# A two-layer transformer kernel whose first attention unit is worked in two parts of keys, with other constants in its ordering program

## The chip, the cores and the metric

The kernel runs on one core of a Trainium2 chip. A core has a matrix engine (TensorE, PE in the profile), a vector engine (VectorE, DVE), a scalar engine for activation functions (ScalarE, ACT), a general engine (GpSimd, POOL), and a queue that here issues all DMA transfers (SyncE, SP). Each engine works through its own instructions in order and waits on semaphores for the others. The metric is the time of one execution in microseconds on the device. Lower is better.

## The reference

Two layers of attention and gated feed-forward with the same weights, over 2048 tokens of width 512, with 32 heads of 16 channels:

```python
def _A_ref(x, wqkv, wo):
    qkv = (x @ wqkv).reshape(B, S, 3, H, Dh).transpose(2, 0, 3, 1, 4)
    q, k, v = qkv[0], qkv[1], qkv[2]
    scores = jnp.einsum("bhqd,bhkd->bhqk", q, k) * (Dh ** -0.5)
    p = _softmax(scores, axis=-1)
    o = jnp.einsum("bhqk,bhkd->bhqd", p, v)
    return o.transpose(0, 2, 1, 3).reshape(B, S, D) @ wo

def _B_ref(x, w_gate, w_up, w_down):
    return (_gelu(x @ w_gate) * (x @ w_up)) @ w_down

x = x + _A_ref(_layernorm(x), A_wqkv, A_wo)
x = x + _B_ref(_layernorm(x), B_w_gate, B_w_up, B_w_down)
x = x + _A_ref(_layernorm(x), A_wqkv, A_wo)
x = x + _B_ref(_layernorm(x), B_w_gate, B_w_up, B_w_down)
```

B is 1, S 2048, D 512, H 32, Dh 16, and the feed-forward is 1792 wide. All inputs and the output are bf16.

## The kernel before, in words

Everything stays on the chip between the first load and the last store. The attention is cut into units: four heads (a group, g from 0 to 7) and a block of 512 tokens as queries (256 in the last two blocks of the second layer). Unit 0 is the first group of the first block. Each unit is worked in two passes over all keys.

Pass 1 finds the row maxima that the softmax needs. TensorE multiplies 128 queries by 512 keys of one head (line 1648), using 32 rows of its array, so that heads lie in row groups of their own. VectorE reduces one or two such PSUM banks to a maximum for each query (line 1663) and writes it into `PM`. A unit of 512 queries has 64 such pieces: 4 tiles of queries, 4 blocks of keys and 4 heads. When all are there, `fin` or `fin_pool` (line 987) takes the maximum over the blocks into `MSEL`, VectorE transposes it into `MT`, and `negmax` (line 1027) has SP move it with four small DMAs (line 1040) into an extra row of `QT`. The scores of pass 2 thus come with the maximum already subtracted.

Pass 2 multiplies 128 keys by the 512 queries (line 1518), ScalarE takes the exponential of one or two banks (line 1494) into `SCR`, and TensorE multiplies that by the values with a column of ones (line 1542), adding up in PSUM bank 7. `nrm` then copies and divides.

There is a third way for part of pass 1, the fold: GpSimd subtracts one key block from another (`kd`, line 1279), TensorE multiplies by the difference (line 1467), ScalarE applies a relu (line 1474), and VectorE adds that to the other block's scores while taking the maximum, in one custom instruction (line 1658). Two blocks are thus done with one reduction on VectorE and one relu on ScalarE.

Around this lie layer norms, projections for keys, queries and values (line 671), transposes (line 816), evacuations of PSUM (line 686 on VectorE, 688 on ScalarE), the output projection, and the feed-forward.

The order of all instructions is worked out in Python when the kernel is built. The program keeps a clock for each engine and at each step chooses what TensorE issues next: the next piece of pass 1, the next pieces of pass 2, both, a piece of a projection or feed-forward, a PV product, or a filler. A filler (line 1687) multiplies zeros into unused columns of a bank, and is issued when TensorE's load over the last 3.4 us falls below a bound. Another sort, the "silent" fillers, fill the gap up to the next event without being counted on the program's clock; they are issued while that clock is between 12 us and `HF`, and only while TensorE is in full-array mode. They share line 1687's matmul.

The choices are steered by 21 constants, among them how far pass 1 may lead before the evacuations go to VectorE (`LAGT`), how far it may lead before a fold is wanted (`FL`), how many tiles of pass 2 go in one step (`NT`), and how much full-array work is cut into one piece (`PIECE`). `PLAN` has one row of these for each 16 steps of pass 1's position; 129 rows cover the run. Reading a row:

```python
SPC, SPLIT, S1C, S2C, OV, LIM, NT, P2B, LAG, LAGT, FL, GL, FX, AHD, DUE, DUEM, PIECE, GP, NPV, PB, OVF = PLAN[stretch[0]]
```

Some units can be split over the keys. Pass 1 of a split unit gives the maximum over its first `n_part` key blocks early (`fin_part`, VectorE reduction and transpose at lines 938 and 940), so that pass 2 can work through those keys; the sums of that part are kept (`keep_part`, line 1059) and later scaled by the exponential of the difference of the two maxima (`merge`, lines 967 to 975) and added (line 1090). Before, the first three units of layer 2 are split, and by `TSPL` the last unit. `HSPL` would split unit 0:

```python
        if HSPL:
            split[0] = 0
            n_part[0] = HNA
            extra[0] = n_qt - 1
```

`HNA` is 3, so the first part has three of four key blocks. `extra` names a second slot of `QT`, into which GpSimd copies the unit's queries (`q_copy`), so that both parts have their maximum in a slot of their own.

Of the kernel before, what the change touches and what calls it, by code (L numbers as in the profile page):

```python
# [310 lines left out]
def _build(nc, x_in, wqkv, wo, wg, wu, wd, out, layer_blocks=((512, 512, 512, 512), (512, 512, 512, 256, 256)),  # L311
# [16 lines left out]
    with es:  # L328
# [1369 lines left out]
        while True:  # L1698
# [3 lines left out]
            if pos["p1"] >= STRETCH * stretch[0]:  # L1702
                if stretch[0] < len(PLAN):
                    SPC, SPLIT, S1C, S2C, OV, LIM, NT, P2B, LAG, LAGT, FL, GL, FX, AHD, DUE, DUEM, PIECE, GP, NPV, PB, OVF = PLAN[stretch[0]]
# [34 lines left out]
            if SP and seam != was[0]:  # L1739
                keep_piece, PIECE = (PIECE, SP) if seam else (0, keep_piece)  # L1740
# [189 lines left out]
```

## Time and profile before

| | |
|---|---|
| median of three runs | 2525.06 us (2524.16 to 2528.22) |
| the profiled execution | 2523.95 us |
| its span, first to last instruction | 2522.2 us |
| granted clock of TensorE | 1.000 |
| TensorE / VectorE / ScalarE / GpSimd busy | 2409.2 / 2403.7 / 2353.2 / 683.9 us |

The profile records one execution. Busy time is the time in which an engine had an instruction under way. Groups are named by line, engine, operation, output and input; "idle before" is the engine's idle time ahead of the group's instructions, and the arrow names what ended it. Neighbouring instructions overlap a little in the records, so a row's mean is some 0.08 us longer than the distance between two in a chain. A line of the table of stretches gives start and end, length, and then the busy time and number of instructions of TensorE, its weight loads, VectorE, ScalarE and GpSimd, the granted clock, and the DMA share and rate.

### The profile page before, as it was taken

What the parts mean: (1) busy time and instruction counts of PE and PEld (TensorE: products, weight loads), DVE (VectorE), ACT (ScalarE), POOL (GpSimd) and SP (SyncE); (2) the same over time, 40 slices, a digit from 0 to 9 for tenths busy, and PEclk for the clock granted to TensorE, in tenths of its full rate; (3) what the DMA queues carried; (4) which work ended last, traced back from release to release, by engine and by line L of the source; (5) the groups of instructions that cost most, each with busy time, mean ns of one, the idle gap of its engine ahead of it and who ended that gap; (6) DMA issues with size and microseconds to landing.
All of it is one profiled execution on the core that took longest, in us unless ns stands there. A gap on an engine that the chain in (4) does not pass through costs nothing.

```text
span 2522.2 us, 68091 instructions
## 1 busy us (share of the span) xinstructions
PE 2409.2 (96%) x29682; PEld 1161.1 (46%) x29881; DVE 2403.7 (95%) x3131; ACT 2353.2 (93%) x3267; POOL 683.9 (27%) x1119
## 2 busy tenths in 40 slices
PE   8999999999999999999999999999999999999999
PEld 3444443445434444344434455434453445534556
DVE  7999999999999999999998999999999999999973
ACT  7799999999999999999979899999999999989996
POOL 4111223321332213431133311341113311442300
PEclk9999999999999999999999999999999999999999
DMA  3110000000000000000000000000000000000000
GB/s 102 38 56 6 4 9 2 4 2 2 8 1 4 2 4 6 3 3 14 13 3 4 17 2 2 8 4 10 2 4 6 6 6 3 4 3 14 2 7 6
DMA packets 27419, 25.07 MB, mean 10 GB/s; under 512 B 9456, under 2 KB 26096, under 8 KB 27120
## 3 DMA queue, kind: packets, MB, share of 16 engines
q1 hardware_dynamic: 27120, 20.71, 2.9%
q8 instruction: 234, 3.83, 0.7%
q14 instruction: 65, 0.53, 0.1%
HBM read 9.70 MB, written 2.10 MB: 5 GB/s over the span
## 4 chain that ended last, share of the span: by engine, by line
PE 42%; DVE 32%; ACT 24%; issue 1%; POOL 0%; ACTq 0%
DVE PM L1663 30%; ACT SCR L1494 22%; PE PS L1648 14%; PE PS L671 12%; PE PS L1542 9%; PE PS L1687 4%; PE PS L1518 3%; ACT SCR L1474 1%; DVE SCR L1658 1%; PE PS L816 1%; ACT AO L1114 0%; PE PS L1467 0%; ACT XNT L688 0%; ACT ATTT L688 0%; ACT SG L688 0%
## 5 line engine op out<-in xcount | busy, mean ns | idle before, releaser
L1663 DVE TENSOR_REDUCE PM<-PS 128x1 f32<-128x512 f32 (+1 forms) x2513 | 2216.6, 944 | 52.0 <-PE PS L1518 24.1
L1494 ACT ACTIVATE SCR<-PS 128x1024 bf16<-128x1024 f32 (+1 forms) x2533 | 2008.2, 899 | 59.2 <-PE PS L1518 43.4
L1648 PE MATMUL PS<-KT,QT 32*128 32x512 bf16 x3923 | 1013.1, 384 | 49.4 <-DVE PM L1663 31.9
L1518 PE MATMUL PS<-QT,KT 32*128 32x512 bf16 (+1 forms) x4608 | 924.0, 360 | 7.5 <-ACT SCR L1494 6.3
L1542 PE MATMUL PS<-VP,SCR 128*128 128x51 bf16 (+1 forms) x16384 | 800.8, 187 | 12.3 <-ACT SCR L1494 8.0
L1542 PEld LDWEIGHTS PS<-VP,SCR 128*128 128x128 bf16 x16384 | 568.3, 96 | 486.8 <-issue 424.8
L1648 PEld LDWEIGHTS PS<-KT,QT 32*128 32x128 bf16 x3923 | 242.2, 91 | 547.8 <-DVE PM L1663 324.5
L1687 PE MATMUL PS<-WV,ZER 128*128 128x240 bf16 x2425 | 425.2, 266 | 4.7 <-ACT SCR L1494 4.5
L1096 POOL TENSOR_TENSOR RL<-ACCS,CM 128x16 f32<-128x16 f32 (+1 forms) x63 | 174.5, 2769 | 564.5 <-ACT ACCS L1086 564.3
L1518 PEld LDWEIGHTS PS<-QT,KT 32*128 32x128 bf16 x4608 | 230.2, 91 | 69.3 <-ACT SCR L1494 42.5
L1687 PEld LDWEIGHTS PS<-WV,ZER 128*128 128x128 bf16 x2425 | 185.1, 96 | 63.9 <-issue 48.5
L1242 POOL TENSOR_TENSOR HT<-HT,AO 128x512 bf16<-128x512 bf16 (+1 forms) x107 | 119.5, 1119 | 236.9 <-ACT AO L1240 236.9
L996 POOL TENSOR_TENSOR PM<-PM 128x16 f32<-128x16 f32 (+2 forms) x130 | 30.2, 232 | 379.1 <-DVE PM L1663 373.9
L1279 POOL TENSOR_TENSOR KD<-KT 128x512 bf16<-128x512 bf16 x72 | 82.9, 1152 | 173.9 <-PE PS L1467 166.0
L671 PE MATMUL PS<-XNT,WU 128*128 128x512 bf16 (+1 forms) x447 | 116.3, 353 | 7.3 <-issue 6.2
L671 PE MATMUL PS<-WD,HT 128*128 128x512 bf16 x381 | 115.5, 380 | 7.2 <-issue 5.4
L671 PE MATMUL PS<-XNT,WG 128*128 128x512 bf16 (+1 forms) x488 | 116.3, 357 | 3.6 <-ACT HT L1221 2.1
L1116 POOL TENSOR_TENSOR X<-X,AO 128x512 f32<-128x512 f32 x46 | 58.3, 1266 | 218.8 <-ACT AO L1114 218.8
L1658 DVE CUSTOM_DVE_ANT_0 SCR<-PS,SCR 128x512 bf16<-128x512 f32 x173 | 111.7, 685 | 3.1 <-PE PS L1467 0.6
L1474 ACT ACTIVATE SCR<-PS 128x512 bf16<-128x512 f32 (+1 forms) x121 | 97.1, 802 | 18.7 <-PE PS L1467 18.3
L1221 ACT ACTIVATE HT<-PS 128x512 bf16<-128x512 f32 (+1 forms) x126 | 69.3, 550 | 36.2 <-PE PS L671 33.4
L671 PEld LDWEIGHTS PS<-XNT,WG 128*128 128x128 bf16 x504 | 39.2, 97 | 55.0 <-issue 29.6
(111 smaller groups left out, 991.0 us busy)
## 6 DMA issues: line engine op xcount, KB each, us to landing
KT<-SG SPq DMA_DIRECT2D x64, 64.0 KB
QT<-MT SPq DMA_DIRECT2D x236, 1.0 KB
QT<-SG SPq DMA_DIRECT2D x56, 64.0 KB
out_dram<-AO SPq DMA_DIRECT2D x16, 128.0 KB, 1.7
WG<-in_B_w_gate_dram SPq DMA_DIRECT2D x4, 448.0 KB, 4.8
WU<-in_B_w_up_dram SPq DMA_DIRECT2D x4, 448.0 KB, 4.7
WD<-in_B_w_down_dram SPq DMA_DIRECT2D x4, 384.0 KB, 4.7
QT<-MT SPq DMA_DIRECT2D x68, 0.5 KB
```

What stands on the lines that cost most here:

```text
L671: ins = e.matmul(out_ap, lhsT=l, rhs=r_, start=(i == 0), stop=(i == n - 1))
L1096: emit("pool", lambda e: e.tensor_tensor(RL[:, s, 0:4 * nq], lsum, CM1[:, 0:4 * nq], op=ALU.pow), r=[("ACCS", s), ("CM1",)], w=[("RL", s)] ...
L1242: emit("pool", lambda e, ft=ft, o=o: e.tensor_tensor(HT[:, ft, 0:n], HT[:, ft, 0:n], AO[:, o, 0:n], op=ALU.mult), r=[("AO", o), ("HT", ft) ...
L1279: emit("pool", lambda e: e.tensor_tensor(KD[:, s, :], KT[:, g, ka * 512:(ka + 1) * 512], KT[:, g, kb * 512:(kb + 1) * 512], op=ALU.subtrac ...
L1474: emit("act", lambda e: e.activation(PT[:, s0:s0 + cnt, :], PS[:, bk:bk + cnt, :], ACTF.Relu), r=bks, w=[("PT", s0 + d) for d in range(cnt ...
L1494: emit("act", lambda e: e.activation(dst, src, ACTF.Exp, scale=DH ** -0.5), r=[BK[bk + i] for i in range(cnt)], w=[("PT", i) for i in slot ...
L1518: ins = e.matmul(bank(bk)[:, i * n:(i + 1) * n], lhsT=KT[32 * j:32 * j + 32, g, kt * 128:(kt + 1) * 128], rhs=QT[32 * j:32 * j + 32, s, 0: ...
L1542: ins = e.matmul(acc, lhsT=PT[:, slot, i * n + qt * 128:i * n + (qt + 1) * 128], rhs=AP(VP, (kt * H + 4 * g + j) * 17, [[NTT * H * 17, 128 ...
L1648: ins = e.matmul(bank(b), lhsT=QT[32 * j:32 * j + 32, s, qt * 128:(qt + 1) * 128], rhs=KT[32 * j:32 * j + 32, g, kb * 512:(kb + 1) * 512], ...
L1658: emit("dve", lambda e, i=i, b=b, sl=sl: e.tensor_tensor_reduce(PT[:, sl, :], bank(b), PT[:, sl, :], 1.0, -3.0e38, ALU.add, ALU.max, po[:, ...
L1663: emit("dve", lambda e: e.tensor_reduce(po, PS[:, bs[0]:bs[0] + cnt, :], axis=AX.X, op=ALU.max), r=bks, w=[("PM", sm) + h[1:] for h in hs] ...
L1687: return e.matmul(PS[:, b, NACC:512], lhsT=ZER[:, :], rhs=WV[:, 0, 0:512 - NACC], start=(b != 7), stop=(b != 7), skip_group_check=True)
```

## The change

Unit 0 is split: its pass 2 can begin with the first 1536 keys once their maxima are there, and its last 512 keys follow as a second part, with the maximum over all keys. The silent fillers are allowed up to 100 us of the program's clock, 60 before. And 106 of the 129 rows of `PLAN` have other constants, some in one of 21, some in nearly all; 23 rows are unchanged. No other code differs.

```diff
 PLAN = [
-    (0.1, 0.1, 0.45, 0.42, 0.3, -0.05, 1, 1, 62, 84, 8, 60, 0.3, 2.0, 0, 2, 2, 1, 7, 1, 0.0),
-    (0.1, 0.1, 0.45, 0.42, 0.3, -0.05, 2, 1, 62, 84, 8, 60, 0.1, 2.0, 0, 2, 2, 2, 7, 1, -0.1),
-    (0.0, 0.1, 0.45, 0.42, 0.3, -0.05, 2, 1, 62, 84, 8, 60, 0.1, 2.0, 0, 2, 2, 2, 7, 1, -0.1),
-    (0.2, 0.1, 0.55, 0.42, 0.3, -0.05, 1, 0, 22, 84, 8, 20, 0.3, 2.0, 0, 6, 1, 2, 9, 1, 0.0),
...
+    (0.1, 0.1, 0.45, 0.42, 0.3, -0.05, 2, 1, 62, 84, 8, 60, 0.3, 2.0, 0, 2, 2, 1, 7, 1, 0.0),
+    (0.1, 0.1, 0.45, 0.22, 0.3, -0.05, 2, 1, 62, 84, 8, 60, 0.3, 2.0, 0, 2, 2, 1, 7, 1, 0.0),
+    (0.15, 0.15, 0.45, 0.42, 0.3, -0.05, 1, 1, 78, 84, 8, 50, 0.3, 2.0, 0, 2, 2, 2, 7, 1, 0.0),
+    (0.2, 0.1, 0.55, 0.82, 0.3, -0.05, 1, 0, 22, 84, 8, 30, 0.4, 2.0, 0, 6, 1, 2, 9, 1, 0.0),
...
-    (0.1, 0.15, 0.45, 0.42, 0.3, 0.05, 1, 1, 94, 92, 8, 60, 0.3, 2.0, 0, 2, 2, 2, 11, 1, 0.0),
-    (0.15, 0.2, 0.25, 0.32, 0.5, -0.05, 1, 1, 86, 84, -2, 80, -0.1, 2.0, 10, -14, 2, 1, 9, 1, 0.0),
...
+    (0.1, 0.15, 0.45, 0.42, 0.3, 0.0, 3, 1, 78, 84, 8, 60, 0.7, 2.5, 10, 2, 2, 2, 3, 1, 0.1),
+    (0.2, 0.15, 0.45, 0.42, 0.3, 0.0, 3, 1, 78, 84, 8, 60, 0.7, 3.5, 10, 2, 2, 2, 3, 1, 0.1),
...
 def _build(nc, x_in, wqkv, wo, wg, wu, wd, out, layer_blocks=((512, 512, 512, 512), (512, 512, 512, 256, 256)),
-           ... NSPL=3, HSPL=0, TSPL=1, HNA=3, TNA=3, ... HV=16, TW=0.95, HF=60, VS=14, ...):
+           ... NSPL=3, HSPL=1, TSPL=1, HNA=3, TNA=3, ... HV=16, TW=0.95, HF=100, VS=14, ...):
```

Where `HV` is named: with unit 0 split, the value projections of the first 12 tiles of keys are due 16 steps of pass 1 earlier.

More of the change, by code (lines that the diff above doesn't have):

```diff
@@ L311, in _build @@
 def _build(nc, x_in, wqkv, wo, wg, wu, wd, out, layer_blocks=((512, 512, 512, 512), (512, 512, 512, 256, 256)),
-           n_ahead=6, n_pre=6, S1C=0.45, S2C=0.42, OV=0.3, PD=80, FDUE=20, LIM=-0.05, NT=1, AHD=2.0, DUEM=2, FDL2=0, OPD=12, URG=0.3, ft_tok=512, n_pt=8, n_qt=8, SPLIT=0.15, SPC=0.1, PVC=47, WARM=0.55, WARML=0.42, NPV=7, BOOST=0.0, LAG=62, LAGT=84, GP=2, SING=0, DUE=0, END=360, LAGE=10, FD=205, FDL=-10, QD=32, KD_=16, VD=20, FL=8, FMAX=6, NKD=2, FLOOK=2, FX=0.3, GF=1, NSPL=3, HSPL=0, TSPL=1, HNA=3, TNA=3, PB=1, OVF=0.0, LNP=0, FNP=1, NSG=3, LNT=12, HV=16, TW=0.95, HF=60, VS=14, SO=1.0, SF=1, SP=0, FAST=1, TG=0, GS=2, P2B=1, PIECE=2, GL=60, GLE=20, HARD=-1e9):
+           n_ahead=6, n_pre=6, S1C=0.45, S2C=0.42, OV=0.3, PD=80, FDUE=20, LIM=-0.05, NT=1, AHD=2.0, DUEM=2, FDL2=0, OPD=12, URG=0.3, ft_tok=512, n_pt=8, n_qt=8, SPLIT=0.15, SPC=0.1, PVC=47, WARM=0.55, WARML=0.42, NPV=7, BOOST=0.0, LAG=62, LAGT=84, GP=2, SING=0, DUE=0, END=360, LAGE=10, FD=205, FDL=-10, QD=32, KD_=16, VD=20, FL=8, FMAX=6, NKD=2, FLOOK=2, FX=0.3, GF=1, NSPL=3, HSPL=1, TSPL=1, HNA=3, TNA=3, PB=1, OVF=0.0, LNP=0, FNP=1, NSG=3, LNT=12, HV=16, TW=0.95, HF=100, VS=14, SO=1.0, SF=1, SP=0, FAST=1, TG=0, GS=2, P2B=1, PIECE=2, GL=60, GLE=20, HARD=-1e9):
     S = x_in.shape[1]
```

192 rows, old and new, of the table PLAN are left out of this document.

## The prediction

> **What bounds the kernel now.** I read the page's busy shares first, then the busy time in stretches of 100 us, then the head in finer stretches, then ScalarE's and VectorE's rows there.
>
> ```profile
> PE 2409.2 (96%) x29682; PEld 1161.1 (46%) x29881; DVE 2403.7 (95%) x3131; ACT 2353.2 (93%) x3267; POOL 683.9 (27%) x1119
> ...
> L1663 DVE TENSOR_REDUCE PM<-PS 128x1 f32<-128x512 f32 (+1 forms) x2513 | 2216.6, 944 | 52.0 <-PE PS L1518 24.1
> L1494 ACT ACTIVATE SCR<-PS 128x1024 bf16<-128x1024 f32 (+1 forms) x2533 | 2008.2, 899 | 59.2 <-PE PS L1518 43.4
> L1687 PE MATMUL PS<-WV,ZER 128*128 128x240 bf16 x2425 | 425.2, 266 | 4.7 <-ACT SCR L1494 4.5
> ```
>
> Two engines are nearly full side by side: VectorE with the row maxima of pass 1 (L1663), ScalarE with the exponentials of pass 2 (L1494). TensorE's 96% contain 425 us of fillers (L1687), so it has room. Idle is 2522.2 - 2403.7 = 118.5 us on VectorE and 169.0 us on ScalarE. The stretches say where:
>
> ```profile
> 0.00:100.00 100.00, 85.75 (x594) 36.93 (x599) 81.19 (x119) 71.94 (x121) 30.70 (x67) 1.00 0.24 69
> 100.00:200.00 100.00, 95.38 (x1313) 49.84 (x1313) 99.18 (x142) 98.23 (x110) 18.83 (x37) 1.00 0.16 55
> 200.00:300.00 100.00, 96.86 (x1283) 49.26 (x1281) 98.65 (x145) 99.26 (x112) 18.02 (x40) 1.00 0.02 6
> ...
> 2400.00:2522.00 122.00, 115.91 (x1556) 69.70 (x1558) 68.73 (x109) 95.36 (x143) 6.56 (x13) 1.00 0.02 7
> ```
>
> The columns are PE, PEld, DVE, ACT, POOL, the granted clock and DMA. The head leaves VectorE 18.8 and ScalarE 28.1 us idle, the last 122 us 53.3 and 26.6; between them the two run at 96 to 99%. So time is gained only where an idle stretch of one is filled and the gain is shared with the other. ScalarE's timeline has the head's largest hole:
>
> ```profile
> 72.02 0.60 ACT L688 ACTIVATE SG<-PS 128x512 bf16<-128x512 f32 x1 [1.13 <-PE PS L671]
> 74.09 1.02 ACT L1474 ACTIVATE SCR<-PS 128x1024 bf16<-128x1024 f32 x1 [1.48 <-PE PS L1467]
> 76.68 1.02 ACT L1474 ACTIVATE SCR<-PS 128x1024 bf16<-128x1024 f32 x1 [1.56 <-PE PS L1467]
> 83.40 5.71 ACT L1494 ACTIVATE SCR<-PS 128x1024 bf16<-128x1024 f32 x7 [5.69 <-PE PS L1518]
> 89.59 22.37 ACT L1494 ACTIVATE SCR<-PS 128x1024 bf16<-128x1024 f32 x24 [0.48 <-PE PS L1518]
> ```
>
> The first exponential starts at 83.40 and ScalarE is then full. It waits for the maxima of unit 0 over all 2048 keys, taken apart on GpSimd, transposed and moved into QT:
>
> ```profile
> 74.78 0.25 POOL L996 TENSOR_TENSOR PM<-PM 128x32 f32<-128x32 f32 x1 [9.88 <-DVE PM L1663]
> ...
> 78.19 0.20 DVE L1000 STREAM_TRANSPOSE MT<-MSEL 128x32 bf16<-128x32 bf16 x1
> ...
> 78.42 2.43 SPq L1040 DMA_DIRECT2D QT<-MT  x4
> ```
>
> The stretches of the head:
>
> ```profile
> 63.60:69.00 5.40, 5.40 (x25) 1.35 (x24) 4.12 (x6) 3.88 (x6) 1.23 (x3) 1.00 0.10 26
> 69.00:83.40 14.40, 12.68 (x85) 5.51 (x83) 14.25 (x25) 3.42 (x6) 2.65 (x8) 1.00 0.08 20
> 83.40:100.00 16.60, 15.71 (x214) 8.35 (x213) 16.55 (x25) 15.95 (x19) 0.00 (x0) 1.00 0.00 1
> ```
>
> From 69 to 83.4 VectorE is full (14.25 of 14.40) and ScalarE works 3.42.
>
> **The split of unit 0.** Unit 0 takes its key blocks one after the other. VectorE's timeline shows four bursts with gaps before 40.31, 53.11 and 64.61, about 9.8 us of maxima each; the third ends at 63.65, the fourth near 74.7. With the split the maxima of the first 1536 keys suffice. Added at once on VectorE: a reduction and a transpose, which the layer turn's split units show at 0.21 each (L938, L940), so MT is ready at 64.1. From MT to the first score took 78.39 to 82.88, or 4.5 us, through four DMAs of 0.61; the first exponential followed 0.5 us later. The part's first exponential thus falls at 69.1, 14.3 us earlier. Other conditions: the values of key tiles 0 to 11 (12 evacuations VP end by 53.6) and a copy of QT on GpSimd (nearest row: 1.15 us for a 512-wide L1279), hidden since GpSimd works 3.9 of 19.8 us there.
>
> What is queued behind the new steps: on SP the four DMAs (2.43 us) stand in a run of 16 key moves, 50.32 to 73.74; the moves behind them belong to later groups, so I cost them at nothing. If that cover is gone, a key move is 2.4 us late and pass 1 with it. On TensorE scores and PV of the part come among the last four key projections (68.8 to 72.0), 0.6 us each; those slip into 72 to 83.4, where fillers take about 6 us.
>
> ScalarE's gain: idle 14.40 - 3.42 = 11.0 us, and 0.48 before 89.59, makes 11.4; the part's 24 exponentials at 0.93 (22.37/24) are 22.4 us of work, enough to fill it. Added on ScalarE: keeping the part (L1059, 0.39) and one small exponential (L970, 0.21), so 10.8 net. Added on VectorE: 0.42 for the part, 0.21 for the full maximum that GpSimd did before, so 0.63. GpSimd gets 0.22 + 0.66 + 0.76 of merging (L967, L975, L1090) and loses 1.5 of the tree; it is 27% busy, nothing.
>
> What the 10.8 us are worth depends on sharing. A fold costs ScalarE a relu (0.92 in the chain) and spares VectorE two paired maxima at 1.14 for two custom instructions at 0.61: 1.06 saved. With x us of folds, ScalarE ends 10.8 - x earlier and VectorE 1.16x - 0.63; equal at x = 5.3, both 5.5 us earlier (about 6 more relus, 12 more custom rows than the 173). Ends: no sharing, and VectorE alone counts, +0.6; ScalarE alone is the bound, as the chain has it from 92 to 112 us, -10.8. I take **-5.5**, since both are at 98 to 99% from 100 to 300 us.
>
> [...] Rows first: two full-array projections among row-tiled scores take 0.54 us in the chain of waits, while fourteen in a row took 3.13, 0.45 for two; with one score matmul the round is 0.86. [...]
>
> **Fillers to 100 us instead of 60.** They go only into idle gaps of TensorE in full-array mode. From 60 to 100 us TensorE is idle 2.8 us in all, the longest gap 0.71, and the granted clock is 1.00 in every stretch. Nothing to gain; at worst each of some 26 fillers of 0.1 delays real work, +2.8. I take 0, the longest gap holding six of them.
>
> **The constants.** 106 of 129 rows differ, 65 of them in no more than five of 21 constants; their means hardly move (tiles at once 1.85 to 1.88, lag 49.4 to 47.2). No row prices this. Its field is the idle between head and tail, 46 us on VectorE and 114 on ScalarE, and how often VectorE takes one bank instead of two: 1276 single maxima at 0.680 against 1237 double ones at 1.216. The nearest stretch is the layer turn, 1240 to 1420 us, 15.1 and 28.7 us idle, mean 22; rows 65 and 66 (counted from 0) are replaced in 16 of 21 constants. Halving or doubling half of that gives -11 and +11. I take **-2**, a tenth of that mean; it is a choice and little more.
>
> **Sum.** The profiled execution took 2523.95 (span 2522.2 and 1.75 around it); -5.5 + 0 - 2.0 gives 2516.5. The median of the three runs is 1.1 above it, so I forecast 2517.5 against 2525.06. No change is what lies within 0.2% (5 us), about what a measurement of this kernel tells apart: 2520.0 to 2530.1.
>
> **Rivals.**
> - *ScalarE's head start stays with ScalarE.* It reaches the maxima sooner and waits there: the wait of L1494 for scores (43.4 us in all) grows by some 10. VectorE's 0.6 is then the sum: 2525.7. For it: only 121 relus in the whole run. Against it: ScalarE at 99% up to 300 us.
> - *The part does not start early,* because its DMAs or the scores wait behind the key moves and projections before 72 us; half the gain and a little delay of pass 1: 2522 to 2525. TensorE is 100% busy in 63.6:69. [...]
> - *The constants find more:* half the turn's idle goes: 2525.06 - 5.5 - 11 = 2508.5.
> - *Slower.* One mechanism: a step of the order puts pass-2 matmuls ahead of the next pair of maxima, and VectorE waits for them; in the rows, L1663 after L1518 is 24.1 us over 66 waits. Where three tiles go at once instead of one (rows 19 and 20 are changed so), each step holds VectorE longer. VectorE is nearly full, so what it waits more is added: with the -5.5 kept, the change is slower than 2530 once these waits grow by 10.5, and by two thirds of their size, 16 us, it takes 2525.1 - 5.5 + 16 = 2535.6. Against it: the mean of that constant hardly moves.
>
> **Chances.** The forecast's mechanism 0.45 (own range 2511 to 2523, of it 0.05 above 2520); first rival 0.13; second 0.07; third 0.15; slower 0.20. Faster: 0.40 + 0.15 = 0.55. Same: 0.05 + 0.13 + 0.07 = 0.25. Slower 0.20. The range 2505 to 2536 takes most of the third and half of the slower case and leaves some 0.15 out; cases of both signs together hold it.
>
> **What would show it.** A reduction of 128x16 from 128x48 near 63.7 us, four moves QT<-MT near 64.2, the first L1494 near 69 instead of 83.40, ScalarE over 12 of 14.4 us busy from 69 to 83.4, and some 185 custom maxima. If these hold and the custom rows don't grow while the wait of L1494 does, sharing failed. If VectorE's idle after L1518 grows past 34 us, the constants did it. Were the first exponential later than 75 us, the second rival holds; a time over 2530 would make the forecast wrong in sign.

## The result, and the profile after

The changed kernel takes 2529.44 us (median of 20 runs, 2526.34 to 2538.93), the kernel before 2524.75 (20 runs beside them, 2523.78 to 2528.22). The ratio is 1.0019, with a 95% interval of 1.0012 to 1.0025. The change is slower by 4.7 us. That is inside the 5 us which the prediction called no change, but the interval excludes no change, and the forecast was 2517.5. The profiled execution took 2530.99 us, with a span of 2529.3 and a mean granted clock of 0.998.

In some profiled executions the granted clock of TensorE falls to 0.50, as for 3.4 us at 56 us or for 10.2 us at 2488; that other long runs with a lower mean clock have such a fall is inferred from the two numbers. Of the 20 runs five are at 2526.3 to 2527.1, seven at 2528.7 to 2529.5 and eight at 2531.0 or more; the mean clock goes down with them, from 1.000 to 0.995. Of the 20 of the kernel before, 16 are near 2524.6 and four near 2528.2. The profiled execution of the changed kernel has such a fall; that of the kernel before has none.

The busy line of the changed kernel's page, and rows of its groups of instructions (columns as before):

```profile
PE 2412.8 (95%) x29669; PEld 1160.4 (46%) x29871; DVE 2402.3 (95%) x3162; ACT 2360.1 (93%) x3285; POOL 680.8 (27%) x1117
...
L1663 DVE TENSOR_REDUCE PM<-PS 128x1 f32<-128x512 f32 (+1 forms) x2516 | 2207.6, 939 | 49.6 <-PE PS L1518 18.3 <-PE PS L1648 13.4 <-PE PS L1467 2.1
L1494 ACT ACTIVATE SCR<-PS 128x1024 bf16<-128x1024 f32 (+1 forms) x2548 | 2012.2, 896 | 64.5 <-PE PS L1518 47.1 <-PE PS L1467 0.3
...
L1658 DVE CUSTOM_DVE_ANT_0 SCR<-PS,SCR 128x512 bf16<-128x512 f32 x183 | 118.0, 686 | 2.8 <-PE PS L1648 1.1 <-PE PS L1518 0.3
...
L1474 ACT ACTIVATE SCR<-PS 128x512 bf16<-128x512 f32 (+1 forms) x127 | 103.0, 812 | 18.5 <-PE PS L1467 17.7 <-PE PS L1648 0.5
```

The two rows of the fold in the kernel before, which the prediction gave only as counts:

```profile
L1658 DVE CUSTOM_DVE_ANT_0 SCR<-PS,SCR 128x512 bf16<-128x512 f32 x173 | 111.7, 685 | 3.1 <-PE PS L1467 0.6 <-PE PS L1648 0.4 <-PE PS L1518 0.2
...
L1474 ACT ACTIVATE SCR<-PS 128x512 bf16<-128x512 f32 (+1 forms) x121 | 97.1, 802 | 18.7 <-PE PS L1467 18.3
```

There are ten more custom maxima and six more relus (the prediction had 12 and 6). VectorE's maxima and custom maxima together are 2.7 us less (9.0 less and 6.3 more); ScalarE is busy 6.9 us more. VectorE's wait for pass-2 scores went down, from 24.1 to 18.3 us: the mechanism that the prediction named for "slower" did not occur.

**The head start came as forecast.** The timeline of the changed kernel, one line each of VectorE, SP's queue and ScalarE:

```profile
64.07 0.21 DVE L938 TENSOR_REDUCE MSB<-PM 128x16 bf16<-128x48 f32 x1
...
64.55 2.42 SPq L1040 DMA_DIRECT2D QT<-MT  x4
...
69.53 1.02 ACT L1494 ACTIVATE SCR<-PS 128x1024 bf16<-128x1024 f32 x1 [1.49 <-PE PS L1518]
```

The first exponential starts at 69.53 instead of 83.40, and ScalarE fills part of the hole (the fourth busy time):

```profile
69.00:83.40 14.40, 14.15 (x125) 5.72 (x126) 13.74 (x22) 10.67 (x18) 0.00 (x0) 1.00 0.09 22
83.40:100.00 16.60, 16.59 (x187) 8.08 (x186) 16.41 (x31) 14.00 (x18) 1.22 (x3) 1.00 0.01 2
```

It works 10.67 us from 69 to 83.4, where it worked 3.42; the prediction had asked for over 12. And it is no longer full behind that: 14.00 of 16.60, before 15.95.

**The gain stopped at the next unit's maxima.** When unit 0's pass 2 is done, ScalarE needs the maxima of unit 1. GpSimd's first step of taking them apart, before and after:

```profile
106.71 0.25 POOL L996 TENSOR_TENSOR PM<-PM 128x32 f32<-128x32 f32 x1 [28.86 <-DVE PM L1663]
```

```profile
106.70 0.25 POOL L996 TENSOR_TENSOR PM<-PM 128x32 f32<-128x32 f32 x1 [18.48 <-DVE PM L1663]
```

They are ready at the same time to 0.01 us. Unit 1's first exponential follows at 114.93, within 0.1 us of unit 0's last; before, it came at 115.19. The last copy of unit 0's sums (L1086) ends at 117.2, before 116.5. So 13.9 us of head start are gone 47 us later. ScalarE's rows from 69 to 114.5 us, each shape by itself, before:

```profile
L1494 ACT ACTIVATE SCR<-PS 128x1024 bf16<-128x1024 f32 x30 | 28.5, 1065 | 6.3 <-PE PS L1518 6.2
L1474 ACT ACTIVATE SCR<-PS 128x1024 bf16<-128x1024 f32 x3 | 3.1, 1046 | 3.0 <-PE PS L1467 3.0
L1494 ACT ACTIVATE SCR<-PS 128x512 bf16<-128x512 f32 x4 | 2.5, 620 | 0.0
```

and after:

```profile
L1494 ACT ACTIVATE SCR<-PS 128x1024 bf16<-128x1024 f32 x23 | 21.8, 1038 | 2.6 <-PE PS L1518 2.5
L1494 ACT ACTIVATE SCR<-PS 128x512 bf16<-128x512 f32 x18 | 10.5, 595 | 4.3 <-PE PS L1518 4.1
L1474 ACT ACTIVATE SCR<-PS 128x1024 bf16<-128x1024 f32 x6 | 6.1, 1032 | 0.4 <-PE PS L1467 0.3
```

The exponentials are 64 banks in both, but now 18 are taken one at a time: 32.3 us of work instead of 31.0, and 6.9 us of waiting instead of 6.3. Three more relus take 3.0 us. With 0.6 for keeping and scaling the part, ScalarE is busy 5.2 us more in this stretch (39.11 against 33.87 of 45.50); the other 6 of the 11.4 us stay idle, in smaller pieces. It waits for scores there, though TensorE has room: fillers take 9.9 of its 22.8 busy us from 69 to 92. VectorE got four more custom maxima for unit 1 (14 against 10 up to 106.7, some 2.1 us spared at the forecast's price), and lost nearly as much by beginning unit 1 at 76.01 instead of 74.61 and by 0.5 us more of idle time up to 106.7.

**Behind the head the two passes drift apart.** The end of each unit's pass 2 (L1086), after minus before: +0.7 us at 117, between -2.8 and +1.0 up to 1100, -6.0 at 1439, -2.0 at 1828, +1.4 at 1990, +2.7 at 2475. The last transpose of pass 1 ends at 2456.4, where it ended at 2470.7. So pass 1 gains 14 us and pass 2, which ends the kernel, loses 2.7. The stretches near the end, before:

```profile
2456.00:2472.00 16.00, 15.45 (x253) 8.49 (x252) 13.41 (x20) 16.00 (x19) 0.40 (x1) 1.00 0.01 2
2472.00:2490.00 18.00, 17.64 (x259) 10.16 (x258) 0.20 (x1) 17.54 (x31) 0.98 (x3) 1.00 0.01 2
```

and after:

```profile
2456.00:2472.00 16.00, 15.36 (x249) 8.50 (x247) 0.52 (x3) 16.00 (x19) 0.40 (x1) 1.00 0.01 2
2472.00:2490.00 18.00, 17.54 (x253) 9.59 (x249) 0.20 (x1) 17.36 (x29) 0.98 (x3) 0.95 0.01 2
```

VectorE (third busy time) works 0.52 us from 2456 to 2472 where it worked 13.41. ScalarE is full in both: what VectorE was spared is of no use there.

**The clock falls once more behind that.** The profiled execution of the changed kernel, in stretches of 5 us:

```profile
2485.00:2490.00 5.00, 5.00 (x54) 2.44 (x52) 0.00 (x0) 4.38 (x11) 0.41 (x1) 0.82 0.01 3
2490.00:2495.00 5.00, 5.00 (x43) 2.63 (x43) 0.00 (x0) 3.33 (x6) 0.00 (x0) 0.50 0.00 0
2495.00:2500.00 5.00, 4.92 (x37) 3.79 (x37) 1.22 (x4) 1.30 (x2) 0.00 (x0) 0.65 0.00 0
```

The lag behind before, +2.7 at 2475, is +7.1 at the end of the span (2529.3 against 2522.2). The fall costs 4.4 us.

### The profile page after: what moved, and what is told of

Same layout as the page of the kernel before. It is cut to its first block, busy times and chain, and to the rows that moved or that the text cites. A ratio compares the mean times of both kernels' runs of the same rounds, so it can differ in the third digit from the quotient of the medians.

```text
span 2529.3 us, 68126 instructions
## 1 busy us (share of the span) xinstructions
PE 2412.8 (95%) x29669; PEld 1160.4 (46%) x29871; DVE 2402.3 (95%) x3162; ACT 2360.1 (93%) x3285; POOL 680.8 (27%) x1117
## 4 chain that ended last, share of the span: by engine, by line
PE 43%; DVE 34%; ACT 22%; issue 1%; DMA 0%; POOL 0%; ACTq 0%; DVEq 0%
DVE PM L1663 33%; ACT SCR L1494 19%; PE PS L1648 14%; PE PS L671 11%; PE PS L1542 9%; PE PS L1687 4%; PE PS L1518 4%; ACT SCR L1474 1%; PE PS L816 0%; ACT AO L1114 0%; DVE SCR L1658 0%; PE PS L1467 0%; ACT ATTT L688 0%; ACT L1494 0%; ACT L1221 0%
## 5 line engine op out<-in xcount | busy, mean ns | idle before, releaser
L1663 DVE TENSOR_REDUCE PM<-PS 128x1 f32<-128x512 f32 (+1 forms) x2516 | 2207.6, 939 | 49.6 <-PE PS L1518 18.3
L1687 PE MATMUL PS<-WV,ZER 128*128 128x240 bf16 x2415 | 436.9, 267 | 4.4 <-ACT SCR L1494 4.4
L671 PE MATMUL PS<-XNT,WU 128*128 128x512 bf16 (+1 forms) x450 | 117.2, 354 | 6.9 <-issue 5.1
L1658 DVE CUSTOM_DVE_ANT_0 SCR<-PS,SCR 128x512 bf16<-128x512 f32 x183 | 118.0, 686 | 2.8 <-PE PS L1648 1.1
L1474 ACT ACTIVATE SCR<-PS 128x512 bf16<-128x512 f32 (+1 forms) x127 | 103.0, 812 | 18.5 <-PE PS L1467 17.7
L1221 ACT ACTIVATE HT<-PS 128x512 bf16<-128x512 f32 (+1 forms) x126 | 69.1, 550 | 33.2 <-PE PS L671 31.0
```

Of the source, the lines that this page charges most:

```text
L671: ins = e.matmul(out_ap, lhsT=l, rhs=r_, start=(i == 0), stop=(i == n - 1))
L1474: emit("act", lambda e: e.activation(PT[:, s0:s0 + cnt, :], PS[:, bk:bk + cnt, :], ACTF.Relu), r=bks, w=[("PT", s0 + d) for d in range(cnt ...
L1658: emit("dve", lambda e, i=i, b=b, sl=sl: e.tensor_tensor_reduce(PT[:, sl, :], bank(b), PT[:, sl, :], 1.0, -3.0e38, ALU.add, ALU.max, po[:, ...
L1663: emit("dve", lambda e: e.tensor_reduce(po, PS[:, bs[0]:bs[0] + cnt, :], axis=AX.X, op=ALU.max), r=bks, w=[("PM", sm) + h[1:] for h in hs] ...
L1687: return e.matmul(PS[:, b, NACC:512], lhsT=ZER[:, :], rhs=WV[:, 0, 0:512 - NACC], start=(b != 7), stop=(b != 7), skip_group_check=True)
```

## The experiments

The kernel before, run beside them, had medians of 2524.25 to 2524.75.

### Each part alone

The split alone, with the constants of before:

```diff
-HSPL=0
+HSPL=1
```

> The kernel before with unit 0 split and nothing else: the old constants, silent fillers to 60 us. Theory A (the split pays about 1 us at most, since what ScalarE gains in the head is spent by 117 us, and constants that were chosen for another head place later work badly): first exponential near 69.5 us, pass 2 of unit 0 ends within 1 us of the 116.1 of before, and the whole is slower than before by 5 to 14 us, lost after 200 us. Rival B (the split is worth its 5.5 us and the new constants lose them): 2517 to 2521, faster than before.

Measured: 2535.68 (5 runs, 2534.72 to 2538.61), ratio 1.0045, interval 1.0032 to 1.0057. Its profiled execution has a fall of the clock at 56 us (mean clock 0.999), and its first exponential is at 72.0, not near 69.5, and unit 0 ends 3.5 us behind before, not within 1 us. The constants alone:

```diff
-PLAN = [ the 129 rows of the kernel before ]
+PLAN = [ the 129 rows of the changed kernel ]
```

> The new constants without the split, silent fillers to 60 us. Theory A (constants and head belong together): slower than the changed kernel, 2530 to 2537. Rival B (the constants alone carry the loss): 5 us slower than the changed kernel, as the split would be worth that, so 2534 to 2536, with the same loss of pass 2 between 1830 and 1950 us as in the changed kernel. Rival C (the constants are neutral, the split costs): 2524 to 2526.

Measured: 2529.94 (11 runs, 2529.31 to 2531.83), ratio 1.0022, interval 1.0013 to 1.0031. The fillers alone:

```diff
-HF=60
+HF=100
```

> The kernel before with silent fillers to 100 us instead of 60, nothing else: the third part of the change alone. Some twenty more fillers stand between 60 and 100 us, where the maxima alone keep VectorE busy. Theory A (they fill idle time and do nothing): 2524.0 to 2525.0, about one run in eight near 2528 as in the kernel before. Theory B (they hold up matmuls that VectorE or ScalarE wait for): the first exponential later than 83.40 us, and 2525.5 to 2527.

Measured: 2524.38 (11 runs, 2521.95 to 2524.77), ratio 0.9996, interval 0.9987 to 1.0005. In the profiled execution the first exponential starts at 84.0 instead of 83.40 and 0.5 us of that stays to the end; the median does not show it.

The fillers do next to nothing. Split and constants each lose alone. With the old constants the split's order parts from the old one, and pass 2 is 12.2 us late from the layer turn (1440 us) to the end. The constants without the split lose in the head, win at the turn and lose more behind it: pass 2 is 4.2 us behind at 658 (in the changed kernel 0.2), 1.0 ahead at 1439, 9.2 behind at 2257 and 7.8 at 2475. The losses don't add up (11.1 and 5.4 against 4.7 together): constants belong to an order. So what the split is worth depends on them. With the old constants it loses 11.1 us; with the new ones, in runs without a fall, it saves 2.9 (2526.7 against 2529.6), since without it their head is slow.

### The split with its head's constants

The changed kernel with the old constants behind the head. Only what is new in the head is left: the split, and rows 0 to 31 that were made for it.

```diff
 PLAN = [
     rows 0 to 31 of the changed kernel
-    rows 32 to 128 of the changed kernel
+    rows 32 to 128 of the kernel before
```

> The split and silent fillers to 100 us, with the new constants for the first 32 rows (to about 540 us) and the old ones for the other 97. Theory A (the loss is made by the new constants behind the head, above all between 1830 and 1950 us, and by the clock in the tail): 2523 to 2526, as before or a little under, pass 2 no more than 1 us from before's from 540 us on. Rival B (the split is worth 5.5 us if constants suit it): 2517 to 2521. Rival D (the new head itself costs): 2527 or more.

Measured: 2526.29 (11 runs), ratio 1.0006, interval 0.9997 to 1.0014. Three runs at a clock of 1.000 took 2523.88, 2523.97 and 2524.15; seven are at 2525.5 to 2526.9 and one at 2531.91. From 660 us on the ends of pass 2 follow those of before at a constant distance, 2.8 to 2.9 us in the profiled run. That run's clock is 0.73 from 55 to 60 us, and the distance is there, a microsecond more or less, from unit 0 on. So the split and the constants made for its head are worth about half a microsecond without that fall, against the old head with its own, and the rows 32 to 128 cost the changed kernel 2 to 2.7 us: its runs without a fall are at 2526.3 to 2527.1, against 2523.9 to 2524.2 here and a median of 2524.72 in the kernel with the hole filled, below.

### Is it the second gate?

The kernel of the last experiment, without folds in the first rows. ScalarE is then free of relus, VectorE has more to do.

```diff
 rows 0 to 3 of PLAN:
-    FL = 8
+    FL = -100
```

> The kernel of the run with the new constants for 32 rows, with folds forbidden in its first four rows (FL -100). Theory A, two gates (pass 2 of unit 1 starts some 5 us after unit 1's maxima, whatever ScalarE has done before, and VectorE sets those): without folds ScalarE ends unit 0 some 8 to 10 us sooner, near 108 us, but unit 1's maxima come 5 to 8 us later than the 106.7 of before, near 113, and pass 2 of unit 1 ends near 157 instead of 151; the whole 5 to 15 us slower than before. Rival B (ScalarE alone is the bound in the head): pass 2 of unit 1 ends 4 us or more sooner than in before, near 146.

Measured: 2528.9 (10 runs, six of them 2528.40 to 2528.93), ratio 1.0021, interval 1.0012 to 1.003. Timeline of its profiled execution (clock 1.000), ScalarE's first exponentials and unit 1's maxima:

```profile
69.44 1.51 ACT L1494 ACTIVATE SCR<-PS 128x1024 bf16<-128x1024 f32 x2 [2.25 <-PE PS L1518]
...
112.56 0.25 POOL L996 TENSOR_TENSOR PM<-PM 128x32 f32<-128x32 f32 x1 [2.90 <-DVE PM L1663]
...
120.29 2.09 ACT L1494 ACTIVATE SCR<-PS 128x1024 bf16<-128x1024 f32 x2 [4.68 <-PE PS L1518]
```

Now unit 0's pass 2 ends at 105.0, 11.5 us ahead of before: most of ScalarE's head start is there. But unit 1's maxima come 5.85 us later, and its first exponential comes 5.1 us later than before, at 120.29, after ScalarE has waited 4.68 us for it. From 620 us to the end pass 2 is 4.8 to 4.9 us behind. The whole is 4.4 us slower, a little less than the 5 to 15 expected, and unit 1 ends at 154.8, not 157. So ScalarE's time in the head had no worth of its own here: it waited at unit 1, and most of what VectorE was late there stayed to the end. With the folds of the changed kernel both gates fall where they were. A setting in between, or more folds, wasn't tried.

### The hole near 55 us

In the split's head TensorE has a gap at 53 to 56 us: the value projections, due earlier, are done by then, and nothing else of the full array is left. From 53 to 56 us it is busy 1.10 us in the changed kernel's profiled execution, 2.80 in that of the kernel before. The fillers go only into full-array mode and leave it. Thirteen more:

```diff
-if HF > now > 12 and mode[0] == "full" and ...:
+if HF > now > 12 and (mode[0] == "full" or 44 < now < 56) and ...:
```

> The same kernel of 32 new rows, with 13 fillers added in TensorE's hole near 55 us, where it waits for VectorE between row-tiled scores. If the hole is what lets the clock fall to 0.50 from 58 to 60 us in the kernel without them: clock 1.000 from 50 to 65 us, 2523.8 to 2524.6 in the median in place of 2526.29, and unit 0's pass 2 ends 2 to 3 us earlier than there. If the fall has another cause: 2526 as before, with the clock below 1 at the same place.

Measured: 2524.72 (11 runs, 2523.88 to 2528.66), nine at a clock of 1.000 where three were; ratio 0.9999, interval 0.999 to 1.0008. In its profile the clock is 1.00 from 50 to 65 us, the first exponential starts at 70.03 and unit 1's maxima come at 107.21. The same edit in the changed kernel:

> The changed kernel with thirteen fillers in TensorE's idle stretches near 55 us, nothing else. Theory A (the runs of the changed kernel near 2529 are those in which the granted clock falls after this hole): the runs at 2528.7 to 2529.5 disappear; what remains is 2526.3 to 2527.2 and, where the clock falls near 2490 us, some 2531; the median 2526.5 to 2527.5. Theory B (the fall in the head has another cause): the runs spread as those of the changed kernel, 2526.3 to 2532, median 2528.5 to 2529.5.

Measured: 2527.27 (11 runs, 2525.23 to 2529.35), ratio 1.001, interval 1.0001 to 1.0019. Seven runs are at 2525.2 to 2527.5, but four at 2528.6 to 2529.4 remain, which should have gone. The profiled one, the longest of them, falls elsewhere:

```profile
710.00:715.00 5.00, 4.06 (x20) 1.18 (x20) 5.00 (x10) 3.95 (x6) 0.00 (x0) 0.92 0.00 0
715.00:720.00 5.00, 4.96 (x48) 2.02 (x46) 3.35 (x6) 3.73 (x7) 1.16 (x1) 0.74 0.00 0
...
2365.00:2370.00 5.00, 5.00 (x60) 2.88 (x57) 4.79 (x8) 4.04 (x7) 3.24 (x9) 0.66 0.00 0
```

So the hole is one place where the clock falls, and not the only one. Of the eight profiled executions with unit 0 split and the hole open, four have the fall at 56 to 57 us; of the three with the hole filled and the three without the split, none has it. These falls thus come with the split's head, though so few executions can't give their rate.

### The fall near 2490 us

The changed kernel with a higher bound for fillers once pass 2 is in its last three units:

```diff
+if p2["i"] >= len(seq) - 3:
+    want, must = max(want, 0.85), max(must, 0.55)
 cool = load < want and ...
```

> The changed kernel with more fillers while the last three parts of pass 2 are worked: the program wants a load of 0.85 there and insists on 0.55. If the granted clock of 0.50 from 2490 to 2495 us costs the changed kernel some 4 us in most of its executions: clock 1.000 in all executions, spread under 1.5 us, 2526 to 2529 (the fillers themselves may take 1 to 2 us). If the clock only mirrors the lower load and costs nothing: 2529 or more, and the spread stays at 5 us and over.

Measured: 2530.43 (11 runs, 2528.25 to 2536.39), ratio 1.0023, interval 1.0014 to 1.0032. The lowest four are at 2528.3 to 2529.0, 2 us above the changed kernel's; six are at 2530.3 to 2531.7, about 2 us above its middle group, and one at 2536.4. A group 4 to 5 us above the lowest, as the changed kernel has it with the fall in the tail, is not there; but the median is no lower, so the fillers cost at least what they save. The clock was not at 1.000 in all executions as expected, and the spread is 8 us: the profiled one falls at 57 us (mean clock 0.999), where these fillers don't reach. The fall in the tail isn't a matter of the new constants either: the profiled execution with the old rows 32 to 128 and the hole filled has it at 2486 us (mean clock 0.998).

### The fillers to 100 us, in the changed kernel

The changed kernel with fillers to 60 us, alone and then side by side with the changed kernel itself:

```diff
-HF=100
+HF=60
```

> The changed kernel with silent fillers only to 60 us, as before: 11 fillers fewer between 60 and 100 us. The prediction put them at 0: 2528.5 to 2530.5, the same as the changed kernel, with as many falls of the clock. Rival: they keep the clock up in the head, then 1 to 3 us slower than the changed kernel.

> The changed kernel once more, beside the next one. Theory A: 2526.3 to 2527.2 where the clock stays at 1.00, 2528.7 to 2529.5 and 2531 to 2532 where it falls once; median near 2529.

> The changed kernel with silent fillers to 60 us as before, instead of 100. Theory A (the eleven further fillers do nothing): the same times as the changed kernel in the same call, within 1.5 us in the median, as many runs with a fallen clock. Theory B (the fillers between 60 and 100 us cost something or bring the clock falls about): median 2 us or more lower than the changed kernel's in this call, with falls in half as many runs or fewer.

Measured: 2526.73 (11 runs, 2526.25 to 2533.85), ratio 1.0013, interval 1.0004 to 1.0022; then 2529.02 for the changed kernel (11 runs, 2526.32 to 2532.90) and 2527.37 for fillers to 60 us (11 runs, 2526.38 to 2534.61). The first lies below the 2528.5 to 2530.5 expected. Without a fall both are at 2526.3 to 2527.4, so the eleven fillers are worth nothing in themselves. With fillers to 100 us, 23 of 31 runs have a fall, with fillers to 60 us 9 of 22; side by side it is 8 and 5 of 11, and the medians differ by 1.65 us, which settles neither theory. The extra fillers stand behind 60 us, so they can't cause the fall at 56. Whether they bring others about, or the difference is chance, stays open.

### A version that beats both

If the loss lies in the constants behind the head, others should win. Starting from the kernel with the hole filled and the old rows 32 to 128, 36 rows were changed (11 of them among rows 0 to 31), wherever the ordering program's own count of the time came out earlier:

```diff
 PLAN: 36 rows other than in the kernel with the hole filled, for example
-    (0.2, 0.15, 0.45, 0.0, 0.9, -0.2, 1, 1, 70, 68, -2, 80, 0.3, 1.0, 30, 6, 2, 2, 8, 1, 0.1),
+    (0.35, 0.2, 0.45, 0.02, 0.1, -0.05, 1, 1, 70, 68, -2, 80, 0.5, 3.0, 10, -14, 1, 1, 8, 1, 0.0),
```

> The split with silent fillers to 100 us and the hole near 55 us filled, the constants taken from the row-0-to-31 kernel and changed in 36 of the rows, wherever the ordering program, on its own count of the time, comes out earlier. Theory A (the constants behind the head are what the changed kernel loses, and another set can win): 2519 to 2521.5, faster than both kernels by 3 to 8 us, pass 1 and pass 2 ending closer together. Theory B (what the ordering program counts is worth nothing on the chip below some 10 us, as the changed kernel's own constants suggest): 2523.5 to 2527, no different from before.

Measured: 2520.71 (11 runs, 2519.84 to 2521.17, none with a fall), the kernel before 2524.25 beside it; ratio 0.9984, interval 0.9976 to 0.9993. It beats both kernels: by 3.5 us, and by 8.3 the changed one's 2529.02 (by 6.0 its runs without a fall). From its page and its stretches near the end:

```profile
PE 2428.5 (96%) x29908; PEld 1162.0 (46%) x29908; DVE 2400.1 (95%) x3132; ACT 2353.8 (93%) x3260; POOL 685.6 (27%) x1123
```

```profile
2456.00:2472.00 16.00, 15.53 (x253) 8.51 (x251) 8.90 (x15) 16.00 (x19) 0.40 (x1) 1.00 0.01 2
2472.00:2490.00 18.00, 17.52 (x242) 10.61 (x239) 1.43 (x5) 15.93 (x30) 0.98 (x3) 1.00 0.01 2
```

VectorE is busy 3.6 us less than before, ScalarE 0.6 more, and pass 1 ends 4.8 us earlier (2465.9) while pass 2 ends 2.8 earlier. In the changed kernel the same numbers are 1.4 less, 6.9 more, 14.3 earlier and 2.7 later. Both engines end earlier, as the prediction had expected of the changed kernel. But the gain isn't made in the head. The first exponential is no earlier (70.77), and from unit 1 to 1100 us pass 2 is within 1.0 us of before's; it is 1.1 ahead at 1593, 1.4 at 1860 and 2.8 at 2475. Whether these constants need the split at all isn't shown: no run has them without it.

## Why the prediction was wrong, point by point

*The split of unit 0, its local working: right up to the first exponential.* The part's reduction was forecast near 63.7 and came at 64.07, the moves near 64.2 and came at 64.55, the first exponential at 69.1 and came at 69.53. The second rival, a part that does not start early, fell. The last two key moves stand behind the second part's four DMAs and end at 80.1, where the last ended at 73.7 before; from 60 to 130 us no engine is shown waiting for keys. Projections two at a time among the scores, which the prediction put at 0.54 us against 0.45 in a row of fourteen, have a price that no run sets apart; the first exponential was 0.4 us later than forecast. What the working had wrong is the filling: 24 exponentials were to make ScalarE full from there on, and it was busy 10.67 of 14.40 us.

*The sharing, -5.5: wrong, and the failed step.* It measured -0.5 to +0.2 us with each head under its own constants (the kernel with the head's constants alone, its runs without a fall, and the one with the hole filled); with the changed kernel's constants throughout the split saved 2.9, with the old ones it lost 11.1. In no pairing is it 5.5. The prediction read "98 to 99% busy" as: ScalarE's time can be traded for VectorE's at any place. The trade has a deadline. Unit 1's pass 2 begins when unit 0's is done and unit 1's maxima are there. Both gates opened near 115 us in both kernels, and with only the first moved forward, in the run without folds, ScalarE stood and waited for the second. To share 5.5 us, VectorE would have had to finish unit 1 5.5 us earlier. It began it 1.4 us later, and was spared some 2.1 us by four more custom maxima. The price of a fold was right (in the changed kernel's chains 0.92 for a relu of two banks, 0.61 for a custom instruction, 1.13 for a paired maximum); the six further relus, put at the whole run's need, had to come within 30 us. Exponentials of single banks, 18 instead of 4, took 1.3 us that the sum did not have: the early scores came one bank at a time.

*The first rival, a head start that stays with ScalarE: right in outcome, in part in mechanism.* It had a chance of 0.13 and a time of 2525.7; the kernel with the split, its head's constants and the hole filled takes 2524.7. ScalarE did not reach unit 1's maxima sooner and wait there, as the rival had it, except in the run without folds. In the changed kernel the head start was used up before, by relus, single banks and short waits, and the wait of the exponentials for scores grew by 3.7 us in the whole run, not by some 10. So the prediction's sign for failed sharing did not appear: the custom maxima did grow, to 183, close to its 185, without a gain.

*The fillers, 0: right* in the kernel before (-0.1 us) and, without a fall, in the changed one.

*The constants, -2: wrong in sign, inside the bounds.* They cost +2.0 to +2.7 us with the split (rows 32 to 128), +5.1 alone (all rows, 2529.6 without a fall). The prediction took them at the mean of the idle time, as if they could only fill it. The rows of the profile show what happened instead: work went from the engine that had time at the end to the one that had none, six more relus against ten custom maxima, and 14 us by which pass 1 ended earlier and that nobody used. That the folds and not the rest of the order did this is argued from the counts; the kernel with other constants, which has four more relus and wins, suggests that their place counts more than their number.

*The slower rival: right in sign, wrong in mechanism.* Its time was 2535.6, and the median did not reach 2530. VectorE's wait for pass-2 scores was to grow past 34 us; it shrank to 18.3. So the sign that the prediction offered for "the constants did it" was no sign of it. What it should have named is the end of pass 1 against the end of pass 2.

*"The granted clock is 1.00 in every stretch": true of one execution, and used as if it were of all.* The runs given had 2528.22 as their longest, 3.2 us above the median; runs of that kernel at 2528 have a mean clock of 0.998. In the changed kernel three runs of four have one. Of the 4.7 us some 2.7 are this (median 2529.4 against 2526.7 without a fall), some 2.3 the constants behind the head, and the split with its head takes off a few tenths at most, besides bringing the fall at 56. Forecast and measurement are 12.2 us apart; the sharing is about 5.2 of them, the constants 4.3, and the falls, for which the sum had no term, 2.7.

## What to carry to other kernels

An engine that is 98% busy is not bound everywhere (ScalarE waited 4.68 us at unit 1 in the run without folds): before a head start is shared out, look up the next point at which the two engines meet, and count what the other one must gain by then. Constants found for one order did not carry over to another here, and their effects did not add up. And when two engines run side by side, compare where their last pieces of shared work end: from VectorE's last transpose of pass 1 to its taking up the last unit's sums (L1076) it is 19.5 us in the kernel before, 21.5 in the fastest, and 36.6 in the changed one with fillers to 60 us and no fall, which says in one number who carries too much.

## What the runs showed of the hardware

In these runs the granted clock also fell while TensorE is recorded as busy. The profiled execution of the changed kernel in stretches of 1 us, where the fall begins:

```profile
2487.00:2488.00 1.00, 1.00 (x15) 0.63 (x14) 0.00 (x0) 0.97 (x3) 0.00 (x0) 1.00 0.06 16
2488.00:2489.00 1.00, 1.00 (x14) 0.68 (x13) 0.00 (x0) 1.00 (x3) 0.00 (x0) 0.61 0.00 0
2489.00:2490.00 1.00, 1.00 (x7) 0.23 (x5) 0.00 (x0) 0.45 (x4) 0.41 (x1) 0.50 0.00 0
```

TensorE is put down as busy 1.00 in each, though the profile models the ends of matmuls, so short idle times could be missing. From 2480 to 2488 us it has 31 score matmuls in 32 rows, 64 of the values with 51 columns and 15 fillers. The fall near 56 us comes after idle time. The changed kernel when it ran again, TensorE's timeline and then its stretches:

```profile
54.07 0.40 PE L1648 MATMUL PS<-KT,QT 32*128 32x512 bf16 x4 [0.53 <-DMA KT<-SG]
55.78 0.51 PE L1648 MATMUL PS<-KT,QT 32*128 32x512 bf16 x2 [1.32 <-DVE PM L1663]
```

```profile
54.00:55.00 1.00, 0.40 (x4) 0.10 (x4) 0.50 (x1) 0.60 (x1) 0.89 (x2) 1.00 0.50 127
55.00:56.00 1.00, 0.21 (x2) 0.09 (x2) 1.00 (x2) 0.00 (x0) 1.00 (x2) 0.96 0.31 79
56.00:57.00 1.00, 1.00 (x8) 0.70 (x7) 1.00 (x2) 0.00 (x0) 0.51 (x1) 0.50 0.48 122
```

Idle time of 0.53 and 1.32 us, with 0.40 us of work between, stands just before the fall in this run; the first profiled execution of the same kernel has a like hole (TensorE busy 0.39, 0.00 and 0.71 us from 53 to 56) and no fall there. The length of a fall follows from the rows, since the clock in it is 0.50 (in every stretch of 1 us from 56 to 59 and from 2489 to 2498): what is missing to 1.00, divided by 0.50. At 2488 it is 0.39 + 9 x 0.50 + 0.23, over 0.50, or 10.2 us; at 56 it is 3.4 us (0.04 + 3 x 0.50 + 0.17), and at 714 and at 2366, with 0.50 taken from the other two, 3.4 us each. One of 3.4 us in the head cost 2.0 to 2.5 us, there at the end of unit 0 and kept, within half a microsecond, to the end of the kernel; one of 10.2 us in the tail 4.4. Three of the four lengths are 3.4 us, and the fourth is three times that. What starts a fall, these runs don't show: from 50 us to the one at 56 the longest idle time in the run shown is 1.32 us, and the stretches from 2484 to 2488 have none.
